# A hand-ordered attention and maxout-FFN kernel: its command list written in a new order, and its last branch laid out anew

## The chip, the cores and the metric

The kernel runs on one core of a Trainium2 chip. The metric is the device time of one execution in microseconds, lower is better. The kernel before ran three times: 202.09, 202.83 and 203.22 us, median 202.83. A profiled execution comes with it; "the profile" and "the trace" below are of that execution.

## The reference

Inputs are q, k, v of 4 batches x 8 heads x 768 positions x 64, a flag per head, and four weights, all float32.

```python
scores = scale * np.matmul(q, k.transpose(0, 1, 3, 2))
causal = rel >= 0                      # rel = query position - key position
stream_keep = causal & (is_sink | in_win)   # first 4 keys, or the last 64
mask = where(is_retrieval[head], causal, stream_keep)
a = softmax(where(mask, scores, -1e9))
x = (a @ v) -> [3072 tokens, 8 heads * 64 = 512]
h = max(x @ w1, x @ w2, x @ w3)        # three 512 x 768 matmuls, elementwise maximum
out = h @ w_out                        # 768 x 512
```

Heads whose flag is set (retrieval heads; 0, 2 and 6 in the data) attend to all earlier keys; the others to 4 sink keys and a window of 64. The result is 3072 x 512 float32.

## The kernel before

The kernel has two programs. The fast one is written for a guess of the flags, `GUESS = (1, 0, 1, 0, 0, 0, 1, 0)`. It also compares the real flags with the guess and checks that all softmax sums are within bounds; from both it makes one integer, `differ`. At its end every engine loads `differ` into a register and branches: if it is not zero, a general program computes everything again. In the data given it is zero, so the branch's body, `general()`, is never entered, but its instructions are there.

**The order.** The fast program is a list of commands, the string tuple `PROGRAM`. They are carried out in the order written; each issues a few instructions to the engines' queues, and each engine works off its own queue in order, waiting where data or buffers are not ready. So the list sets the order of the work on every engine, and letters in the commands (d, a, p: VectorE, ScalarE, GpSimd) set which engine does a copy, a cast or a mask. The commands:

- `hl half hp n`: loads of q and k of batch 0 for n head pairs, half a sequence each, by SP's DMA queue (line 185). `cast` (L199) makes them float16, `turnp` turns them by PE transposes (L217) and copies them to the tile KQ (L220).
- `load b quad`: loads of q and k of the later batches by GpSimd's DMA queue. `turn b quad i part` turns a quarter with one VectorE 32 x 32 transpose (L251); eight of them make a batch.
- `load_v b half` loads V by SP's queue; `v` (L436) and `y` (L448, L450) copy it as float16 to the tiles va and vx.
- `kx0` and `kx` (L476, L481, L488) gather far and sink keys. `cleark j` clears the two kx tiles of one parity (L465); `clear j` clears va's ones column and vx (L346 to L348).
- `strip n0 n1` copies mask blocks into the strip that masks are read from, 14 VectorE copies each (L333).
- `s0 half u pairs...` and `s b s`: score matmuls (L526, L597) into one of two PSUM buffers, and the exp on ScalarE (L546, L614). `k0` (L558) and `k` (L627) multiply a mask into the result, on VectorE or GpSimd.
- `av b half hp`: the attention times V for two heads (L646), reciprocal of the sums (L651) and scaling to x (L653) on VectorE. With D at the end, x goes transposed to xT by a DMA on SP's queue; without it, the command `x` does that by PE (L669) and a copy (L672).
- `w i`: a weight's load with a cast, by GpSimd's DMA queue (L361; w 3 is w_out).
- `f e`: one unit of the FFN. For each batch and half (384 tokens) there are 18 units of four matmuls (L387, a [128 x 384] block of one of the three products), whose result is copied to acc (L395) or taken as a maximum (L397), and 3 output blocks of six matmuls (L412), a copy (L418) and a store. For batch 0 all units of the first weight come first, then those of the second; later they alternate. The PSUM results of units, transposes and av share a ring of four banks.
- `flags`, `check`, `verdict` (L680 to L710): the comparison of flags, the check of sums, and the matmul and addition that write `differ`.
- `gs i` and `gp half hp`: tiny copies on SP's or GpSimd's queue that hold the queue until a weight or a load has landed. `idle n`: n matmuls on zeros (L295).

FFN units stand between the commands of the next batch's attention, so that PE always has something to do while the other engines prepare. L779 loads `differ`; L780 is the branch; rows of L941 belong to the closing behind it, where the engines wait for each other.

## Time and profile before

| | us |
|---|---|
| three runs, median | 202.83 |
| the profiled execution | 202.28 |
| its span, first to last instruction | 200.2 |
| PE busy | 180.6 |
| VectorE (DVE) busy | 152.4 |
| ScalarE (ACT) busy | 99.4 |
| GpSimd (POOL) busy | 72.3 |
| last matmul ends | 193.4 |
| first FFN unit on PE | 32.2 |

Times in the trace count from the first instruction of the span. A row of a group gives the source line, the engine, the operation, the tile written and the tile read, the number of instructions and either total and mean ns, or least, median and largest ns with the first and last start. A row of the waits reads: engine and tile that waited, what it waited for, us in total, how often, the longest. In a row of stretches each engine's busy us stands with its number of instructions; the last three columns are the clock granted to PE (1.00 is full), the mean busy share of the DMA engines, and GB/s.

### The profile page before, as it was taken

The numbers are of one execution on the slowest core, as the hardware profiler recorded it, in microseconds if no ns is written. First come the engines' busy times: TensorE is split into PE (matmuls) and PEld (weight loads), VectorE is DVE, ScalarE is ACT, GpSimd is POOL, SyncE is SP. The second block draws the span as 40 slices with busy tenths as digits, with TensorE's granted clock in tenths as the row PEclk, the third lists the DMA queues.
The fourth block names the chain that finished last, engine by engine and source line by source line (L and its number), as shares of the span: only waits on it lengthen the run. The fifth ranks groups of instructions, "written<-read, shape, count | busy, mean of one in ns | idle before, by whom it ended". The sixth has DMA issues, their size and how long they took to land.

```text
span 200.2 us, 4763 instructions
## 1 busy us (share of the span) xinstructions
PE 180.6 (90%) x1833; PEld 106.2 (53%) x1833; DVE 152.4 (76%) x357; ACT 99.4 (50%) x170; POOL 72.3 (36%) x111
## 2 busy tenths in 40 slices
PE   0297798999999999999999999999999999999960
PEld 0244365565555644567556645574566467655530
DVE  4897569999797899998479999793667469877800
ACT  2359758723867666174765584537556350000030
POOL 6134724446798215077092049013571030000000
PEclk9999559999999999999999999999999999999996
DMA  5999999999498958996498141014201511340040
GB/s 143 321 166 210 255 203 202 211 142 208 71 212 201 184 102 182 291 230 128 143 233 159 20 144 57 0 24 123 96 0 23 151 65 22 62 157 4 0 160 11
DMA packets 48424, 26.63 MB, mean 133 GB/s; under 512 B 37259, under 2 KB 43915, under 8 KB 48395
## 3 DMA queue, kind: packets, MB, share of 16 engines
...
## 4 chain that ended last, share of the span: by engine, by line
PE 71%; DVE 11%; DMA 8%; issue 3%; ACT 3%; SPq 2%; DVEq 0%; ACTq 0%
PE yy L387 39%; PE yy L412 11%; PE oacc L646 6%; PE st L597 6%; DMA qs<-in_q_dram 6%; PE yst L387 3%; DVE x L653 2%; DMA xT<-x 2%; DVE hT L397 2%; DVE KQ L251 2%; SPq L185 2%; PE st L526 1%; PE tr L217 1%; DVE acc L397 1%; PE yst L412 1%
## 5 line engine op out<-in xcount | busy, mean ns | idle before, releaser
L614 ACT ACTIVATE pt<-st 128x1024 f16<-128x1024 f32 (+2 forms) x51 | 43.5, 907 | 28.0 <-PE st L597 26.4
L627 POOL TENSOR_TENSOR pt<-pt,strip 128x512 f16<-128x512 f16 (+4 forms) x36 | 35.7, 1008 | 55.4 <-ACT pt L614 52.4
L387 PE MATMUL yy<-xT,w2t 128*128 128x384 f16 x180 | 36.0, 326 | 0.4 <-ACT ot L418 0.4
L387 PE MATMUL yy<-xT,w0t 128*128 128x384 f16 x180 | 35.8, 326 | 0.4 <-DMA xT<-x 0.2
L387 PE MATMUL yy<-xT,w1t 128*128 128x384 f16 x180 | 35.2, 326 | 0.2 <-DVE x L653 0.2
L397 DVE TENSOR_TENSOR acc<-yy,acc 128x384 f16<-128x384 f32 x45 | 24.9, 558 | 10.3 <-PE yy L387 4.7
L412 PE MATMUL yy<-woutt,hT 128*128 128x512 f16 (+1 forms) x138 | 31.4, 375 | 0.4 <-DVE hT L397 0.4
L397 DVE TENSOR_TENSOR hT<-yy,acc 128x384 f16<-128x384 f32 x45 | 24.6, 554 | 3.8 <-PE yy L387 1.6
L395 ACT CAST acc<-yy 128x384 f16<-128x384 f32 x26 | 12.4, 486 | 28.1 <-PE yy L387 28.1
L251 DVE STREAM_TRANSPOSE KQ<-kq 128x384 f32<-128x384 f32 x24 | 25.5, 1132 | 0.0
L387 PEld LDWEIGHTS <-w0t 128*128 128x128 f16 x192 | 18.1, 98 | 13.4 <-issue 1.0
L387 PEld LDWEIGHTS <-w1t 128*128 128x128 f16 x192 | 18.1, 98 | 12.9 <-issue 1.1
L387 PEld LDWEIGHTS <-w2t 128*128 128x128 f16 x192 | 17.5, 97 | 12.4 <-issue 1.3
L412 PEld LDWEIGHTS <-hT 128*128 128x128 f16 x150 | 14.0, 98 | 16.1 <-DVE hT L397 1.7
L546 ACT ACTIVATE pt<-st 128x1024 f16<-128x1024 f32 (+4 forms) x28 | 16.2, 636 | 10.1 <-PE st L526 9.8
L646 PEld LDWEIGHTS <-pt 128*128 128x128 f16 x472 | 18.0, 100 | 3.0 <-issue 0.4
L646 PE MATMUL oacc<-va,pt 128*128 128x65 f16 x392 | 19.0, 197 | 0.0
L653 DVE TENSOR_TENSOR x<-oacc,sums 128x384 f16<-128x384 f32 x32 | 17.8, 557 | 1.1
L627 DVE TENSOR_TENSOR pt<-pt,strip 128x256 f16<-128x256 f16 (+4 forms) x33 | 13.9, 437 | 5.6 <-ACT pt L614 5.6
L597 PE MATMUL st<-KQ 32*128 32x128 f16 (+2 forms) x342 | 15.1, 257 | 0.0
L597 PEld LDWEIGHTS <-KQ 32*128 32x128 f16 x342 | 8.8, 92 | 6.8 <-issue 5.6
L646 PE MATMUL oacc<-vx,pt 128*128 128x65 f16 x80 | 12.3, 193 | 0.0
...
## 6 DMA issues: line engine op xcount, KB each, us to landing
...
```

The costliest lines, as they stand in the source:

```text
L185: eng.dma_start(out=st[:, h : h + 2], in_=src[0, 2 * hp + h : 2 * hp + h + 2, half * HALF : (half + 1) * HALF].rearrange("h (p j) d -> p h ...
L251: nc.vector.transpose(out=dst.rearrange("c (p j) -> c j p", j=n)[:, j0:j1], in_=src.rearrange("c (j i) -> c j i", i=R),)
L387: nc.tensor.matmul(yy[:, 0:HALF], w_t[wi][:, ks, ni * P : (ni + 1) * P], xT[b, half, ks].rearrange("p a t -> p (a t)"), start=(ks == 0), s ...
L395: copy_out[0](out=acc[ni], in_=yy[:, 0:HALF])
L397: nc.vector.tensor_tensor(out=acc[ni] if wi == 1 else hT[ni], in0=yy[:, 0:HALF], in1=acc[ni], op=ALU.max)
L412: nc.tensor.matmul(yo[:, 0:n], hT[ns][:, tb * P : (tb + 1) * P], woutt[:, ns, c : c + n], start=(ns == 0), stop=(ns == NNB - 1),)
L546: nc.scalar.activation(out=pts[0, half, hp, u][:, r0:r1, c0:c1], in_=sts[hp][:, r0:r1, c0:c1], func=AF.Exp, scale=sc,)
L597: nc.tensor.matmul(sts["XY"[g // 2]][:, g % 2, c0 : c0 + n * P], KQ[rows, 0, ki * P : (ki + 1) * P] if kind == "p" else kx[b % 2][quad][ro ...
L614: nc.scalar.activation(out=pts[b, s, xy][:, r0:r1, c0:c1], in_=st[:, r0:r1, c0:c1], func=AF.Exp, scale=sc,)
L627: engine.tensor_tensor(out=x, in0=x, in1=m, op=ALU.mult)
L646: nc.tensor.matmul(o[:, i, r, 0 : D + 1], at[b, h, kind, ki, qi], vv[:, 0 : D + 1], start=(n == 0), stop=(n == len(todo) - 1), skip_group_ ...
L653: nc.vector.tensor_tensor(out=x, in0=o[:, :, :, 0:D], in1=rc.unsqueeze(3).to_broadcast([P, HB, 2, D]), op=ALU.mult,)
```

## The change

Three things change. The list is written anew: the same commands in another order, with engines of copies, casts and masks assigned anew, and the two `idle` commands at other places. A command `read` loads `differ` to a register of all five engines, and a command `hint` on all five announces the branch at the end with its register. And the branch is laid out the other way round: the empty arm, which is the one taken, no longer follows the branch directly with a jump past `general()` behind it; it stands behind `general()`, ahead of the closing, and is reached by the branch's own jump.

By letters: masks `k` on VectorE/GpSimd 33/36 before and 26/43 after; `k0` 9/8 and 1/16; `f` on ScalarE/VectorE 90/78 and 96/72; `v` on ScalarE/VectorE/GpSimd 11/11/10 and 9/13/10; `y` 5/12/10 and 10/6/11.

```diff
-    "clear 1, flags, hl 0 1 1 ss, clear 0, cast 0 0 pp, turnp 0 0 dd, cleark 0, hl 0 2 2 ss",
-    "strip 0 14, cast 0 2 aa, cast 0 1 ap, turnp 0 1 d, kx0 0 0 a, s0 0 0 0, hl 1 0 2 ss",
-    "cast 1 0 dd, turnp 0 2 ad, turnp 1 0 da, cleark 1, load_v 0 0 0 4, cast 1 1 ap, idle 2",
-    "kx0 0 1 a, s0 0 0 1, cast 0 3 dd, s0 0 1 0, s0 0 1 1, strip 14 28, kx0 1 0 p, load_v 0 0 4 4",
-    "v 0 0 3 d, hl 1 2 2 ss, v 0 0 2 d, turnp 0 3 aa, cast 1 2 dd, load 1 0, s0 1 1 0, s0 0 1 3",
...
-    "y 0 0 5:8:2 s d, s0 0 0 3, turnp 1 3 da, s0 0 0 2, turnp 1 2 da, k0 0 1 1 d, s0 1 3 1, w 0",
-    "kx0 1 3 d, v 0 0 1 p, x 0 0 0 a, av 0 0 3, y 0 0 4:5:1 r p, av 0 0 1, s0 1 0 1",
-    "y 0 0 4:5:1 s p, av 0 0 2, w 1, s0 1 1 3, w 2, turn 1 0 1 0, load_v 0 1, x 0 0 1 d",
...
-    "f a, load 1 1, turn 1 0 0 0, f d, f a, k0 1 0 0 d, kx0 1 2 p, s0 1 1 1, k0 1 0 1 d",
...
-    "f a, f a, f a, v 0 1 0 a, w 3, av 0 1 0 D, v 0 1 2 a, v 0 1 1 p, k0 3 3 0 p, av 0 1 1 D, f d",
-    "s0 1 2 3, k0 2 1 2 p, turn 1 1 0 0, s0 1 0 2, turn 1 1 0 1, k0 2 0 2 p, turn 1 1 1 0",
-    "turn 1 1 1 1, f d, v 0 1 3 a, idle 8, f d, f a, f a, s 1 1, load_v 1 0, k0 3 1 1 p, av 0 1 3",
...
-    "f d, f a, gp 1 2, k 3 5 X 0 d, av 3 1 2 D, f a, gs 0, f d, k 3 3 X 0 p, f d, av 3 1 0 D",
-    "av 3 1 1 D, f d, av 3 1 3 D, f d, f a, f a, f d, f d, f d, f d, f d, f d, f a, f a, f a, f d",
-    "f d, check, f d, f d, f a, f a, f a, f d, f d, f d, gs 1, verdict, f a, f a, f d, f a, f a",
+    "cast 0 0 aa, turnp 0 0 ad, hl 0 1 1 ss, clear 0, cleark 0, cast 0 1 aa, hl 0 2 2 ss",
+    "cast 0 2 da, load_v 0 0 0 4, kx0 0 0 a, s0 0 1 0, turnp 0 1 d, hl 1 0 2 ss, cast 1 0 dp",
+    "s0 0 0 0, turnp 0 2 da, s0 0 1 1, idle 8, w 0, kx0 0 1 d, cast 1 1 dp, cast 0 3 da",
+    "turnp 0 3 dd, y 0 0 1:4:2 r a, load 1 0, kx0 0 2 a, s0 0 0 2, load_v 0 0 4 4, kx0 0 3 p",
...
+    "turnp 1 0 da, clear 1, kx0 1 0 p, s0 0 0 3, av 0 0 0, s0 0 1 2, av 0 0 1, turnp 1 1 a, w 1",
+    "hl 1 2 2 ss, w 2, cast 1 3 pp, load_v 0 1, turnp 1 3 aa, x 0 0 1 d, cast 1 2 dd, kx0 1 1 p",
+    "s0 0 1 3, y 0 0 4:5:1 s a, s0 1 3 3, cleark 1, y 0 0 5:8:2 s p, gs 1, av 0 0 3, v 0 0 2 p",
+    "av 0 0 2, x 0 0 0 a, kx0 1 3 d, s0 1 0 1, x 0 0 3 a, strip 14 28, load 1 1, x 0 0 2 a",
+    "load_v 1 0, strip 0 14, s0 1 2 1, w 3, turnp 1 2 aa, kx0 1 2 d, k0 3 3 0 p, s0 1 0 3, f d",
...
+    "k0 3 1 1 p, f d, k0 3 0 1 p, idle 2, turn 1 1 0 1, turn 1 1 0 0, kx 1 1 a, k0 3 1 0 p",
+    "k0 2 0 2 p, k0 0 0 1 p, f d, gp 1 2, v 0 1 3 p, k0 3 0 0 p, f a, turn 1 1 1 0, turn 1 1 1 1",
...
+    "f a, s 2 1, k 2 1 X 1 p, turn 3 0 0 0, f a, av 1 1 0 D, turn 3 0 1 0, f d, av 1 1 3 D",
...
+    "k 3 6 Y 0 d, f a, k 3 4 X 1 d, f a, f d, flags, f d, f a, f a, f a, k 3 7 X 0 p, k 3 4 Y 0 p",
...
+    "f d, verdict, f d, f a, f a, read, hint, f a, f d, f d, f d, f d, f a, f a, f d, gs 0, f d",
+    "f d, f a, f a, f a, f a, f a, f a",
...
+    def read():
+        found["n"] = nc.values_load(differ[0:1, 0:1], min_val=0, max_val=1 << 20)
...
+        read=read,
+        hint=lambda: tc.mark_branch_hint_location("last", found["n"], [mybir.EngineType.SP, mybir.EngineType.PE, mybir.EngineType.Activation, mybir.EngineType.DVE, mybir.EngineType.Pool]),
...
-    return differ
+    return found["n"]
...
-        differ = fast(
+        n = fast(
...
-        n = nc.values_load(differ[0:1, 0:1], min_val=0, max_val=1 << 20)
-        with tc.If(n > 0, preferred_fallthrough_block=False):
+        with tc.If(n > 0, preferred_fallthrough_block=True, label="last"):
             general(tc, nc, q, k, v, is_retrieval, int(n_sink), int(window), w_t, woutt, out, xs_dram)
```

75 rows, old and new, of the table PROGRAM are left out of this document.

## Prediction, made before the changed kernel had run

> **What bounds the kernel now.** I read the page first: the shares of the engines and the chain that ended last.
>
> ```profile
> PE 180.6 (90%) x1833; PEld 106.2 (53%) x1833; DVE 152.4 (76%) x357; ACT 99.4 (50%) x170; POOL 72.3 (36%) x111
> ...
> PE 71%; DVE 11%; DMA 8%; issue 3%; ACT 3%; SPq 2%; DVEq 0%; ACTq 0%
> ```
>
> TensorE is the bound. The number of matmuls does not change, so only the time in which PE stands still, or runs at a lower clock, can be won or lost. The table of busy time in stretches tells where that is.
>
> ```profile
> 10.00:15.00 5.00, 4.76 (x30) 2.28 (x28) 4.89 (x16) 2.78 (x6) 1.73 (x4) 1.00 0.96 167
> 15.00:20.00 5.00, 3.59 (x38) 2.06 (x34) 3.52 (x18) 4.54 (x12) 2.32 (x6) 0.91 1.00 209
> 20.00:25.00 5.00, 3.99 (x31) 1.77 (x29) 2.67 (x7) 3.78 (x8) 3.82 (x7) 0.50 1.20 255
> 25.00:30.00 5.00, 4.93 (x52) 3.16 (x53) 3.15 (x11) 2.64 (x5) 1.06 (x3) 0.56 1.15 202
> ...
> 30.00:50.00 20.00, 19.50 (x209) 11.73 (x210) 19.68 (x41) 10.95 (x21) 9.94 (x16) 1.00 1.10 191
> ...
> 50.00:193.40 143.40, 142.02 (x1472) 83.81 (x1469) 111.26 (x235) 71.34 (x113) 49.48 (x64) 1.00 0.48 110
> ...
> 195.00:201.00 6.00, 0.00 (x0) 0.00 (x0) 0.00 (x0) 0.00 (x0) 0.00 (x0) 0.63 0.06 16
> ```
>
> Columns: stretch, length, then PE, PEld, DVE, ACT, POOL busy; last the granted clock, the DMA share, GB/s. Three things are to be seen. Before 30 us DMA is full (0.96 to 1.20) while no engine is. From 30 to 50 DVE has 19.68 of 20.00: it sets the pace. From 50 to 193.4 PE lacks 143.40 - 142.02 = 1.38 us, and after 195 nothing computes for 5.2 us. Why DVE enters its full stretch late is in the waits and in the weight's DMA:
>
> ```profile
> DVE qn L199 <- DMA qs<-in_q_dram: 3.7, 1, 3.7
> ...
> L361 POOL DMA_DIRECT2D w0t<-in_moe_w_dram x1: 816/816/816, 20.4 to 20.4; - x1
> ...
> DMA to landing us min/median/max: 9.5/9.5/9.5
> ...
> L251 DVE STREAM_TRANSPOSE KQ<-kq x8: 1097/1122/1161, 31.3 to 47.0; 128x384 f32<-128x384 f32 x8
> ...
> L333 DVE COPY strip<-kb x28: 129/181/600, 9.2 to 17.3; 128x128 f16<-128x128 f16 x28
> ```
>
> The first weight lands at 20.4 + 9.5 = 29.9; the eighth transpose of batch 1 ends at 47.0 + 1.1 = 48.1. The end is in the rows of the branch (line 780) and of the closing (line 941):
>
> ```profile
> L780 PEldq COMPARE_BRANCH  x2: 95/1892/3688, 191.2 to 193.5; - x2
> L780 SPq COMPARE_BRANCH  x2: 38/48/57, 193.5 to 195.8; - x2
> L780 ACTq COMPARE_BRANCH  x2: 38/44/49, 194.8 to 194.9; - x2
> ...
> L941 SPq EVENT_SEMAPHORE  x14: 17/28/28, 198.5 to 200.1; - x14
> ...
> L941 ACTq DRAIN  x2: 8/43/78, 195.4 to 199.6; - x2
> L941 PEldq DRAIN  x2: 8/40/73, 197.3 to 199.7; - x2
> ```
>
> SP jumps at 195.8 and does its next instruction at 198.5: 2.7 us with nothing between. PE's jump takes 3.7 (193.5 to 197.3). ACT jumps at 194.9 and goes on at 195.4: 0.5.
>
> The sums below start from the profiled execution, 202.28 us (span 200.2, 2.08 around it); the median of the runs is 202.83, 0.55 or 0.3% above it, and the runs go from 202.09 to 203.22, so the profiled one is of the quicker sort: I add 0.2 at the end.
>
> **The end.** The empty arm now stands just ahead of the closing, the jump into it is announced by the hint, and the second, unconditional jump goes. If the target is there when SP jumps, SP takes ACT's 0.5 in place of 2.7: 2.2 us. What SP does behind it (198.5 to 200.1) waits for PE's closing too, and PE's 3.7 was over at 197.3; if its jump shrinks alike, PE is done by 194.0 and holds nobody. The last output's landing (SP waits until 195.7) is untouched. No row shows a hint here. Ends: 0 (the target is fetched all the same) and 2.7 + 0.1 for the jump that goes; I take 2.3, nearest to ACT's row.
>
> The early **read** of the flag stands three units behind the verdict. In before DVE wrote the flag at 188.6, 0.7 after the verdict's matmul at 187.9, and a load of it took 0.49 on PE: 1.2 us, under which lie three units of 4 x 0.326 / 2 = 0.65, that is 1.95 (the chain shows 0.65 a unit). PE's load could be issued as soon as its queue reaches it, ahead of the matmuls that still wait, and then holds those behind it: bound 0 to 0.5, I take 0. On DVE (0.82) and ACT (0.48) the load is hidden by 190 to 195, where they are busy 0.46 and 1.54 of 5.
>
> **The start.** Removed from the early part: both strip fills and one clear (kx of batch 1). They go behind `x 0 0 1`, the turn of the second head pair for the FFN. The weight w0 is issued after the cast of the first pair of the second half, about 13 instead of 20.4, so it lands near 22.5 by its own 9.5. It no longer sets the first unit (32.2 in before); x does, and that needs the q of the last pairs of the second half, which landed at 22.2 (end of the 3.7 wait). POOL then casts k and q (0.51 each), PE turns them, ACT copies (0.48 each): `x 0 0 1` ends on DVE near 23.0. I follow DVE from there to the eighth transpose, in order, by the rows of before:
> - 8 transposes x 1.122 = 9.0; 12 FFN copies and maxima x 0.556 = 6.7; two of av (0.189 + 0.557) = 1.5; two casts x 0.54 = 1.1; two clears of kx x 0.485 = 1.0; four small copies and masks about 0.8: 20.1.
> - 28 strip copies: their two groups took 1.4 + 2.3 = 3.7 wall.
>
> Successive rows of DVE overlap: between 32.6 and 48.1 the durations sum to 17.0 in 15.6 us, so 20.1 counts 20.1 x 0.92 = 18.4. With 3.7 that is 22.1 us. In before DVE was idle for about 4 us between the landing at 22.2 and its eighth transpose (25 to 30 alone shows 1.85); there PE stood at clock 0.50 and they waited for each other. Now the strips and the clears, which wait for nobody, lie in that place; I leave 1.2 of idle. The eighth transpose then ends at 23.0 + 22.1 + 1.2 = 46.3, against 48.1, and PE's list ahead of it holds 16 units instead of 13 (+1.95), less two av's of two head pairs (2 x 0.62) and a score block (0.1): 0.6 more. Gain 1.8 + 0.6 = 2.4.
> Ends: if DVE idles 4 us as before, and x comes 1 us late, it is 2.4 - 2.8 - 1.0 = -1.4. On the good side landings bind: the last quarter of batch 1 landed at 42.3 and as many bytes stand ahead of it as before, so two transposes behind it end at 44.5: 4.2. w1 (34.5) and w2 (38.6) would be wanted near 34.5 and 39, just covered.
>
> **Queues.** SP is now held by its gate on w1 (to 34.5); behind it stand only the loads of V for batch 1, used past 47. POOL takes 16 of 17 masks of the first batch and 43 of 69 later (36 before), at 1.01 against 0.44 on DVE: POOL has 49.5 of 143.4 busy, so 7 us fit, and each takes 0.44 off DVE. A mask that is late holds an av by 0.6; I count nothing, up to +0.5.
>
> **The middle.** PE's 1.38 us of standing lie at 60 to 80 (0.83) and 100 to 120 (0.47), where the transposes of batches 2 and 3 fill DVE (14.74 of 16 from 64 to 80). The transposes are spread anew; the tightest place left is batch 1's second half, two av's with two transposes of batch 3 between them (2.2 on DVE under 1.3 of units). I take 0.5 won of the 1.38; ends +1.4 and -1.5 (that pair uncovered and one landing late).
>
> Sum: 202.28 - 2.3 - 2.4 - 0.5 = 197.1, and with the 0.2, **197.3**.
>
> [...]
>
> **Rivals.**
> 1. The hint brings nothing: the gap of 2.7 stays. For it: no row shows a hint working, and 15 units lie between it and the jump. Against: ACT, DVE and POOL jump in 0.5, so the target need not be far in itself. 197.3 + 2.3 = 199.6.
> 2. The start gains nothing: DVE idles as in before (4 us), 2.8 more: 197.3 + 2.8 = 200.1. For it: clock 0.50 and DMA 1.2 may hold in 20 to 30 as before. Against: the strips fill it.
> 3. Slower: w0 passes the last q and k of the second half on DMA. It has 512 x 768 x 4 B = 1.57 MB; at the 335 GB/s of the fullest stretch 4.7 us. If all of it goes ahead, x comes at 27.7, and with 4 us idle the eighth transpose ends at 53.8: 5.7 - 0.6 = 5.1 lost, 202.28 + 5.1 - 2.8 = 204.6. It decides once x and the idle time together come 5.2 us later than the forecast's 23.0 + 1.2, for then the 2.4, the 2.3 and the 0.5 are used up. Against: q and k go by SP's queue, w0 by POOL's, and they share.
> 4. Better: landings alone bind the start (4.2 in place of 2.4): 195.5.
>
> Both 1 and 2: 202.4, no change.
>
> **Chances.** Forecast 0.43, rival 1 0.16, rival 2 0.17, both 0.07, rival 3 0.12, rival 4 0.05. About 0.5% (1 us, 201.8 to 203.8) is what can be told from no change: faster 0.81, same 0.07, slower 0.12. The range runs from rival 4 with the end at its own bound (195.5 - 0.5 = 195.0) to the two failures together (202.4); outside lie rival 3 and a little below.
>
> **What would show it.** End: SP's closing semaphores within 1 us of its second-last branch row, PE's within 1 us too; else rival 1. Start: w0 issued near 13 and landed by 23; `x 0 0 1` on DVE by 23; eighth transpose by 46.3; PE full from there. Rival 3: the wait of the cast for qs ends past 25. Middle: PE busy in 50 to its last matmul within 0.9 of that stretch. What would make me wrong most: a cold clock for longer than 19 to 29, or DVE's long stretch idling on landings.

## The result, and the profile after

The changed kernel took 214.18 us (median of 4 runs, 213.44 to 215.35), the kernel before 202.81 beside it: a ratio of 1.0567, interval 1.0536 to 1.0598. It is 11.4 us slower where 197.3 was forecast, and outside of the range. The profiled execution took 215.35, its span is 213.6. (In e7, e10, e13 and e18 below some executions were over 1.5% longer than the fastest of their kernel; the ratios leave those out, so there they do not agree with the medians, and the traces of e10 and e18 are of such executions.)

The page of the kernel after, its busy times and the shares of the chain that ended last:

```profile
PE 183.2 (86%) x1833; PEld 105.9 (50%) x1833; DVE 143.4 (67%) x337; ACT 101.5 (48%) x175; POOL 86.4 (40%) x126
...
PE 67%; DMA 18%; DVE 7%; SPq 2%; issue 2%; ACT 1%; POOL 1%; POOLq 0%; DVEq 0%
```

TensorE has the same 1833 matmuls and is busy 2.6 us longer with them (some ran at a lower clock: in the units of the first weight up to 0.528 us instead of 0.326). DVE's share of the chain fell from 11% to 7%, as one would expect from the masks that left it. But DMA's rose from 8% to 18%: what is new on the chain is transfers. The chain names them by line (first row), and its longest pieces by start and length:

```profile
by line: PE yy L388 40.6%; DMA qs<-in_q_dram 9.8%; PE yy L413 9.1%; DMA xT<-x 7.8%; PE oacc L647 5.3%; PE st L598 5.2%; DVE KQ L252 2.9%; PE yst L388 2.8%; issue 1.6%; PE st L527 1.4%; SPq L186 1.1%; DVE x L654 1.1%; SPq L275 0.9%; DVE hT L
...
15.32 13.38 DMA qs<-in_q_dram
57.74 10.36 DMA xT<-x
```

Two transfers: one load of q that took 13.4 us, and one DMA transpose of x that took 10.4. Both are to be found in the busy times by stretches (columns as in the prediction):

```profile
15.00:20.00 5.00, 4.21 (x62) 2.64 (x60) 4.50 (x14) 4.31 (x8) 3.73 (x7) 1.00 1.06 201
20.00:25.00 5.00, 0.50 (x3) 0.24 (x3) 0.46 (x1) 1.18 (x3) 0.50 (x1) 0.61 1.10 227
25.00:30.00 5.00, 0.58 (x6) 0.59 (x7) 0.00 (x0) 0.05 (x1) 1.02 (x3) 0.50 1.15 210
30.00:35.00 5.00, 4.76 (x47) 2.68 (x44) 4.48 (x18) 3.90 (x9) 3.70 (x7) 0.50 1.17 208
...
60.00:80.00 20.00, 14.92 (x149) 7.79 (x151) 8.57 (x18) 10.20 (x15) 6.90 (x7) 0.83 0.84 153
...
140.00:160.00 20.00, 18.24 (x223) 11.20 (x220) 13.14 (x31) 10.94 (x18) 7.22 (x7) 1.00 0.22 61
```

From 20 to 30 PE does 1.08 of 10 us (before: 8.92, at half clock), and no other engine does more than a fifth either: everybody waits, with DMA full. PE's granted clock is 0.50 until 38.1 (its row from 30 to 35 shows 4.76 us of work at 0.50). From 60 to 80 PE lacks 5.1 us (before 0.8). From 140 to 160 it lacks 1.8 (before nothing). What PE waited for in the first 70 us, the longest two:

```profile
PE tr L218 <- POOL qn L200: 5.7, 1, 5.7
PE yy L388 <- DMA xT<-x: 5.1, 1, 5.1
```

**The first hole.** The loads of q by SP's queue and the weights' DMAs on POOL's:

```profile
L186 SPq DMA_DIRECT2D qs<-in_q_dram x7: 368/467/469, 2.2 to 15.3; - x7
...
DMA to landing us min/median/max: 3.6/4.5/13.4
```

```profile
L362 POOL DMA_DIRECT2D w0t<-in_moe_w_dram x1: 962/962/962, 13.4 to 13.4; - x1
...
L362 POOL DMA_DIRECT2D w1t<-in_moe_w_dram x1: 747/747/747, 17.9 to 17.9; - x1
...
L362 POOL DMA_DIRECT2D w2t<-in_moe_w_dram x1: 755/755/755, 18.6 to 18.6; - x1
```

The last q was issued at 15.3, as in before (15.6), and landed at 28.7; in before the q that VectorE waited for landed at 22.2, and the last one was there by 24.5, when its cast began without a wait. All three weights are issued by 18.6; in before none of them was before 20.4. So `x 0 0 1` ends at 30.6 and the first FFN unit starts at 36.3 (32.2 in before), although w0 had landed at 22.9. Between 0 and 60 us the copy of `x 0 0 1` on DVE waited for its turn on PE:

```profile
DVE xT L673 <- PE tr L670: 9.8, 1, 9.8
```

That turn does not read the late q. What it reads, the scaled x of the second head pair, was written by DVE at 20.5. But in the list `turnp 1 3`, the turn of that q, stands ahead of `x 0 0 1`, and PE did them in that order: the turn of q at 29.41, that of x at 29.71. So the q holds the first unit by its place in the queue alone.

**The second hole**, 63.08 to 68.15: the DMA transposes of x for the second half, and the loads of batch 2's k and q on POOL's queue:

```profile
L660 SPq DMA_TRANSPOSE xT<-x x3: 1267/1267/1468, 57.7 to 60.7; - x3
...
DMA to landing us min/median/max: 8.2/9.1/10.4
```

```profile
L237 POOL DMA_DIRECT2D kq<-in_k_dram x3: 530/549/596, 55.8 to 57.4; - x3
L237 POOL DMA_DIRECT2D kq<-in_q_dram x3: 525/545/548, 56.4 to 58.4; - x3
```

The six loads were issued from 55.8 on, the last one at 58.4, the transposes at 57.7, 59.3 and 60.7. The last load landed at 67.90, and the transposes at 68.11, 68.45 and 68.84. The first transpose even landed behind two loads that were issued 0.2 and 0.7 us after it (they landed at 65.51 and 67.90). In before the loads were spread from 52.9 to 63.7, and the transposes were quicker:

```profile
L236 POOL DMA_DIRECT2D kq<-in_k_dram x3: 524/556/598, 52.9 to 62.7; - x3
L236 POOL DMA_DIRECT2D kq<-in_q_dram x3: 497/520/536, 53.5 to 63.7; - x3
...
L659 SPq DMA_TRANSPOSE xT<-x x5: 1181/1206/1966, 52.2 to 73.1; - x5
...
DMA to landing us min/median/max: 2.3/3.9/4.6
```

**The end:**

```profile
L785 SPq EVENT_SEMAPHORE  x7: 17/17/17, 211.5 to 211.9; - x7
...
L785 PEldq COMPARE_BRANCH  x1: 417/417/417, 204.8 to 204.8; - x1
...
L785 SPq COMPARE_BRANCH  x1: 73/73/73, 208.2 to 208.2; - x1
```

PE's jump shrank from 3.7 to 0.42. SP's did not: 208.2 to 211.5, 3.3 us. But SP now jumps while the last output is still on its way (landed by 211.0), so only 0.5 to 0.8 of it shows, counted from that landing. From the last matmul (207.6) to the end of the span there are 6.0 us; in before 200.2 - 193.4 = 6.8.

### The profile page after: what moved, and what is told of

Same layout as the page of the kernel before. It is cut to its first block, busy times and chain, and to the rows that moved or that the text cites. A ratio compares the mean times of both kernels' runs of the same rounds, so it can differ in the third digit from the quotient of the medians.

```text
span 213.6 us, 4761 instructions
## 1 busy us (share of the span) xinstructions
PE 183.2 (86%) x1833; PEld 105.9 (50%) x1833; DVE 143.4 (67%) x337; ACT 101.5 (48%) x175; POOL 86.4 (40%) x126
## 4 chain that ended last, share of the span: by engine, by line
PE 67%; DMA 18%; DVE 7%; SPq 2%; issue 2%; ACT 1%; POOL 1%; POOLq 0%; DVEq 0%
PE yy L388 41%; DMA qs<-in_q_dram 10%; PE yy L413 9%; DMA xT<-x 8%; PE oacc L647 5%; PE st L598 5%; DVE KQ L252 3%; PE yst L388 3%; PE st L527 1%; SPq L186 1%; DVE x L654 1%; SPq L275 1%; DVE hT L398 1%; PE yst L413 1%; ACT pt L547 1%
## 5 line engine op out<-in xcount | busy, mean ns | idle before, releaser
L628 POOL TENSOR_TENSOR pt<-pt,strip 128x512 f16<-128x512 f16 (+5 forms) x43 | 43.2, 1022 | 62.4 <-ACT pt L615 62.1
L388 PE MATMUL yy<-xT,w0t 128*128 128x384 f16 x180 | 38.7, 344 | 7.1 <-DMA xT<-x 7.1
L388 PE MATMUL yy<-xT,w1t 128*128 128x384 f16 x180 | 35.7, 326 | 0.0
L388 PE MATMUL yy<-xT,w2t 128*128 128x384 f16 x180 | 35.5, 326 | 0.1
L396 ACT CAST acc<-yy 128x384 f16<-128x384 f32 x32 | 15.4, 482 | 38.9 <-PE yy L388 32.9
L398 DVE TENSOR_TENSOR acc<-yy,acc 128x384 f16<-128x384 f32 x45 | 24.9, 560 | 12.3 <-PE yy L388 8.8
L647 PEld LDWEIGHTS <-pt 128*128 128x128 f16 x472 | 17.9, 99 | 5.3 <-issue 1.2
L647 PE MATMUL oacc<-va,pt 128*128 128x65 f16 x392 | 19.6, 196 | 1.0 <-ACT pt L547 1.0
L654 DVE TENSOR_TENSOR x<-oacc,sums 128x384 f16<-128x384 f32 x32 | 17.9, 558 | 1.2
L559 POOL TENSOR_TENSOR pt<-pt,strip 128x128 f16<-128x128 f16 (+3 forms) x16 | 12.6, 815 | 6.5 <-ACT pt L547 3.9
L396 DVE CAST acc<-yy 128x384 f16<-128x384 f32 x13 | 7.2, 555 | 11.3 <-PE yy L388 11.3
L419 ACT COPY ot<-yy 128x512 f32<-128x512 f32 x14 | 8.1, 588 | 12.0 <-PE yy L413 8.5
```

Source lines behind the costliest of these rows:

```text
L388: nc.tensor.matmul(yy[:, 0:HALF], w_t[wi][:, ks, ni * P : (ni + 1) * P], xT[b, half, ks].rearrange("p a t -> p (a t)"), start=(ks == 0), s ...
L396: copy_out[0](out=acc[ni], in_=yy[:, 0:HALF])
L398: nc.vector.tensor_tensor(out=acc[ni] if wi == 1 else hT[ni], in0=yy[:, 0:HALF], in1=acc[ni], op=ALU.max)
L559: engine.tensor_tensor(out=x, in0=x, in1=m if r < 2 else m.to_broadcast([P, 2, n, P]), op=ALU.mult)
L628: engine.tensor_tensor(out=x, in0=x, in1=m, op=ALU.mult)
L647: nc.tensor.matmul(o[:, i, r, 0 : D + 1], at[b, h, kind, ki, qi], vv[:, 0 : D + 1], start=(n == 0), stop=(n == len(todo) - 1), skip_group_ ...
```

## The experiments

The theory after the result: three weights issued early take the DMA from the last loads of the second half (the first hole), and the loads of batch 2 take it from the transposes (the second). Rivals: one of the two is enough; the later order of the list or the new engines cost by themselves; DVE's strips behind `x` set the start; the new end costs.

### Each hole by itself

**e1: only w0 later**

```diff
-    "s0 0 0 0, turnp 0 2 da, s0 0 1 1, idle 8, w 0, kx0 0 1 d, cast 1 1 dp, cast 0 3 da",
+    "s0 0 0 0, turnp 0 2 da, s0 0 1 1, idle 8, kx0 0 1 d, cast 1 1 dp, cast 0 3 da",
...
-    "turnp 1 0 da, clear 1, kx0 1 0 p, s0 0 0 3, av 0 0 0, s0 0 1 2, av 0 0 1, turnp 1 1 a, w 1",
+    "turnp 1 0 da, clear 1, kx0 1 0 p, s0 0 0 3, av 0 0 0, s0 0 1 2, av 0 0 1, turnp 1 1 a, w 0, w 1",
```

> The changed kernel (214.2) with one command moved: the load of w0 goes from behind the cast of the first pair to just ahead of the load of w1, behind the loads of the last q and k of the second half. Theory (w0 goes ahead of those q and k on DMA and makes them land late): the last q lands by about 23 in place of 28.7, PE's hole of 5.7 us at 23.8 to 29.4 is gone or under 1 us, and the time falls by 4 to 6, to 208 to 210. Rival (they are late because three loads of V now stand ahead on SP's own queue): the landing stays at 28 to 29 and the time at 213 to 215.

Measured: 214.55 us, 1.0536 (1.0464 to 1.0609): no gain that can be told. The last q took 10.9 instead of 13.4 and landed at 25.6, and the first unit started at 33.2 instead of 36.3. But little of it was left at the end: at the transposes PE now stood for 6.1 us instead of 5.1. So w0 is a part of the first hole, and to mend that part alone brings nothing that can be told.

**e2 and e3: the loads of batch 2 later in the list.** e2 moves both halves of them behind the last av of the first half and its turn; e3 only the second half.

```diff
-    "av 0 1 3, load 2 0, v 0 1 0 a, av 0 1 0 D, load 2 1, v 0 1 2 a, s 1 1, k 1 1 X 0 p",
-    "k 1 1 X 1 d, av 0 1 1 D, av 0 1 2 D, x 0 1 3 d, f d, s 1 0, k 1 0 X 0 d, load_v 1 1",
+    "av 0 1 3, v 0 1 0 a, av 0 1 0 D, v 0 1 2 a, s 1 1, k 1 1 X 0 p",
+    "k 1 1 X 1 d, av 0 1 1 D, av 0 1 2 D, x 0 1 3 d, f d, load 2 0, load 2 1, s 1 0, k 1 0 X 0 d, load_v 1 1",
```

> The changed kernel with both loads of batch 2 moved from ahead of the three DMA transposes of batch 0's second half to behind them and one FFN unit. Theory (a DMA transpose lands only after all loads that were issued before it): the transposes land within 4 us of their issue (10.4 in the changed kernel), PE's hole of 5.1 us at 63.1 to 68.2 is gone, and the time falls by 4 to 5, to 209 to 210. Rival (the DMA engines are simply full, whatever the order): a hole of some 3 to 5 us stays at that place or opens a little later, where batch 2 is turned: 212 to 214.

The edit of e3, against the kernel after:

```diff
-    "av 0 1 3, load 2 0, v 0 1 0 a, av 0 1 0 D, load 2 1, v 0 1 2 a, s 1 1, k 1 1 X 0 p",
-    "k 1 1 X 1 d, av 0 1 1 D, av 0 1 2 D, x 0 1 3 d, f d, s 1 0, k 1 0 X 0 d, load_v 1 1",
+    "av 0 1 3, load 2 0, v 0 1 0 a, av 0 1 0 D, v 0 1 2 a, s 1 1, k 1 1 X 0 p",
+    "k 1 1 X 1 d, av 0 1 1 D, av 0 1 2 D, x 0 1 3 d, f d, load 2 1, s 1 0, k 1 0 X 0 d, load_v 1 1",
```

> As the run before, but only the second load of batch 2 (four DMAs of the six) is moved behind the transposes. If a transpose waits for whatever was issued ahead of it, it lands just behind the last piece of the first load (62.9 in the changed kernel), so about 63 to 64, and the hole shrinks from 5.1 to 0 to 1: 209.5 to 210.5. If it only shares the DMA engines with what is under way at any time, the moved load, issued 3 us later, still slows it: a hole of 2 to 4 us and 211 to 213.

Measured: e2 218.5, 1.0742 (1.0681 to 1.0803); e3 215.87, 1.0678 (1.0607 to 1.075). Neither is better than the kernel after (1.0567), and e2 is worse. The loads of k in e2, by the tile that they write, and the transposes by theirs:

```profile
L237 POOL DMA_DIRECT2D kq<-in_k_dram x3: 530/549/596, 58.6 to 60.2; - x3
```

```profile
DMA to landing us min/median/max: 2.4/6.8/10.1
```

The loads had moved in the list, but hardly in time: POOL had nothing ahead of them that waits, so it ran ahead of PE and issued them at 58.6 to 61.2, now between the three transposes (57.5, 58.9, 60.2). The first transpose, issued 1.1 us ahead of the first load, took 2.4; the second, between the loads, 6.8; the third 10.1. In e3 the first, issued 0.03 us ahead of a load, took 5.9, and the second and third 10.4 and 9.3. So e2 is no test of "loads away". e3 was to tell whether a transpose waits only for loads issued ahead of it, for then they had to land by 63 to 64: they landed at up to 68.2, so that is not so. The forecast for sharing (211 to 213, with PE standing for 2 to 4) missed as well: PE stood for 5.9.

**e5: the loads behind an instruction that waits.** `k 1 2 X 0 p` is a mask on POOL that needs a result of PE.

```diff
-    "av 0 1 3, load 2 0, v 0 1 0 a, av 0 1 0 D, load 2 1, v 0 1 2 a, s 1 1, k 1 1 X 0 p",
+    "av 0 1 3, v 0 1 0 a, av 0 1 0 D, v 0 1 2 a, s 1 1, k 1 1 X 0 p",
...
-    "v 1 0 1 a, v 1 0 2 p, f a, k 1 0 X 1 d, f d, s 1 2, k 1 2 Y 0 d, f a, k 1 2 X 0 p, f a, f a",
+    "v 1 0 1 a, v 1 0 2 p, f a, k 1 0 X 1 d, f d, s 1 2, k 1 2 Y 0 d, f a, k 1 2 X 0 p, load 2 0, load 2 1, f a, f a",
```

> The changed kernel with both loads of batch 2 behind a mask of batch 1 on POOL's queue, which waits for an exp (its mask started at 64.3), so that they are issued near 65 and not between the transposes as in the two runs before, where POOL ran ahead. Theory (a DMA transpose lands only behind all that was issued before it): all three transposes land 2 to 4 us after their issue, by 65; PE's hole of 5.1 us at 63 is gone or under 0.7; 209 to 210.5, if nothing later waits for the loads (first needed at 78). Rival (the full DMA engines set it): the hole comes back at the turns of batch 2 or at the later transposes, 212 to 215.

Measured: 211.3, 1.0392 (1.0308 to 1.0476). The loads were issued near 65, and the transposes:

```profile
L660 SPq DMA_TRANSPOSE xT<-x x3: 1179/1207/1312, 57.4 to 60.1; - x3
...
DMA to landing us min/median/max: 2.3/2.3/2.4
```

The second hole is gone, and its cause is shown: the loads of batch 2 beside the transposes. The gain is 1.75% (3.5 us) and not 5, and a new hole of 2.3 us stands at 71.1, behind a copy of V on DVE that took 3.95 us (see e7).

**e6: the three weights behind the casts of the last pair of the second half**, that is, once its q has landed.

```diff
-    "s0 0 0 0, turnp 0 2 da, s0 0 1 1, idle 8, w 0, kx0 0 1 d, cast 1 1 dp, cast 0 3 da",
+    "s0 0 0 0, turnp 0 2 da, s0 0 1 1, idle 8, kx0 0 1 d, cast 1 1 dp, cast 0 3 da",
...
-    "turnp 1 0 da, clear 1, kx0 1 0 p, s0 0 0 3, av 0 0 0, s0 0 1 2, av 0 0 1, turnp 1 1 a, w 1",
-    "hl 1 2 2 ss, w 2, cast 1 3 pp, load_v 0 1, turnp 1 3 aa, x 0 0 1 d, cast 1 2 dd, kx0 1 1 p",
+    "turnp 1 0 da, clear 1, kx0 1 0 p, s0 0 0 3, av 0 0 0, s0 0 1 2, av 0 0 1, turnp 1 1 a",
+    "hl 1 2 2 ss, cast 1 3 pp, w 0, w 1, w 2, load_v 0 1, turnp 1 3 aa, x 0 0 1 d, cast 1 2 dd, kx0 1 1 p",
```

> The changed kernel with the loads of all three first weights behind the cast that waits for the last q and k of the second half. Theory (not w0 alone but the three weights, 4.7 MB issued by 19.4 us, share DMA with these q and k): the last q lands at 22 to 23.5 (28.7 in the changed kernel, 25.6 with w0 moved alone), x is turned by 25, the first unit starts near 33 to 34 as w0 lands about 33, against 36.3; the hole at 20 to 29 shrinks by 5 us. If the hole at 63 stays as it is: 209 to 211; if it takes the gain back, because the loads of batch 2 are then issued earlier against the transposes, as with w0 moved alone: 212 to 214. Rival (V's loads ahead on SP's queue hold q): q lands at 25 or later, 213 to 215.

Measured: 213.79, 1.0504 (1.0423 to 1.0584); by the intervals that is not told apart from the kernel after. The loads of q and PE's longest waits:

```profile
DMA to landing us min/median/max: 3.6/4.9/8.9
```

```profile
PE yy L388 <- DMA xT<-x: 5.9, 1, 5.9
PE tr L218 <- POOL qn L200: 4.2, 1, 4.2
```

With no weight beside it the longest q takes 8.9 and lands at 24.0. So the last q took 13.4 with w0 issued at 13.4, 10.9 with all three weights issued after 17.7 (e1), and 8.9 with none beside it. The first unit starts at 32.4 instead of 36.3; and the wait at the transposes is 5.9 us long instead of 5.1, as in e1. The price is that the weights now land late, at 31.8, 35.4 and 39.4.

**e7: e5 and e6 together**

> The two edits before together. If these are the two causes of the loss and do not share a cause, the time falls by the sum of theirs, to 203.5 to 206; what is left over 202.8 less the shorter end is the new order's own. If something else in the start (clock, strips on DVE) costs as much: 207 or more.

Measured: 208.54, 1.0239 (1.0158 to 1.032). By the ratios e5 took 1.75% off, e6 0.6%, both 3.3%. Each is uncertain by some 0.8, so that they are worth more together than singly is not shown by the times; e6's trace, with its longer wait at the second hole, is what speaks for it. The time is still above the forecast of 203.5 to 206, so something else costs as well. A new hole of PE stands at 67.5 (2.3 us). A small copy of V on DVE, and the masks on POOL between 64 and 70:

```profile
L449 DVE CAST vx<-vs x1: 3964/3964/3964, 65.2 to 65.2; 64x128 f16<-64x128 f32 x1
```

```profile
L628 POOL TENSOR_TENSOR pt<-pt,strip 128x512 f16<-128x512 f16 (+2 forms) x4 | 4.5, 1149 | 0.0
```

The copy took 3.96 us, where the same copy takes 0.22 elsewhere. During it POOL ran four masks one directly behind the other, from 65.3 to 69.7; the copy, begun at 65.2, ended at 69.2, half a microsecond before the recorded end of the last of them (as in e5).

**e10: e7 with that copy on ScalarE**

```diff
-    "y 1 0 4:5:1 r d, k 1 0 Y 0 p, f d, av 1 0 0 D, load_v 2 0, f d, turn 2 0 0 0, s 1 5, f a",
+    "y 1 0 4:5:1 r a, k 1 0 Y 0 p, f d, av 1 0 0 D, load_v 2 0, f d, turn 2 0 0 0, s 1 5, f a",
```

> The kernel with both edits (e7, 208.5) and one copy of V (64 x 128, y 1 0 4:5:1 r) on ScalarE in place of VectorE. In e7 this copy took 3.96 us on VectorE at 65.3, 0.22 in the changed kernel, while GpSimd ran four masks end to end from 65.3 to 69.7, and PE then stood 2.3 us. Theory (VectorE was shut out by GpSimd's masks, which holding the loads had moved there): without the copy no VectorE row there is over 1 us, PE's hole at 67.5 is gone, 206 to 207. Rival (chance of this row, or another VectorE operation is shut out in its place): a hole of 1 to 2.5 us stays near there, 207.5 to 209.

Measured: 205.84, 1.0127 (1.0084 to 1.017). The copy takes 0.3 on ScalarE, the hole at 67.5 is gone, and PE is busy 20.00 of 20.00 from 60 to 80. One letter is worth 1.1% by the middle of the two ratios, 2.3 us; their intervals just meet (1.0158 and 1.017), so the hole that is gone from the trace, 2.3 us too, says it more surely than the times. The same four masks ran here (66.0 to 70.5). That masks on POOL do not hold all of DVE's work is seen in the kernel after: its 32 scalings to x, which read PSUM, took 0.557 to 0.559 us each, three of them wholly beside masks. With the two holes and the one that opened behind them taken out, 1.3% of the 5.7% remain.

**e4: the kernel before, with w0 issued early and nothing else**

```diff
-    "cast 1 0 dd, turnp 0 2 ad, turnp 1 0 da, cleark 1, load_v 0 0 0 4, cast 1 1 ap, idle 2",
+    "cast 1 0 dd, turnp 0 2 ad, turnp 1 0 da, cleark 1, load_v 0 0 0 4, cast 1 1 ap, w 0, idle 2",
...
-    "y 0 0 5:8:2 s d, s0 0 0 3, turnp 1 3 da, s0 0 0 2, turnp 1 2 da, k0 0 1 1 d, s0 1 3 1, w 0",
+    "y 0 0 5:8:2 s d, s0 0 0 3, turnp 1 3 da, s0 0 0 2, turnp 1 2 da, k0 0 1 1 d, s0 1 3 1",
```

> The kernel before (202.8) with one command moved, the load of w0 put where the change has it, behind the early casts of the second half (issued near 12 in place of 20.4). Theory (w0 delays the last q and k): these land 4 to 6 us later than 22.8, the first FFN unit starts later than 32.2 although its weight is there earlier, and the time rises by 3 to 5, to 206 to 208. Rival (the order of the rest is what costs): 202 to 204, as the weight comes earlier and q and k as before.

Measured: 204.98, 1.0118 (1.0073 to 1.0163). The weight and the first unit:

```profile
L361 POOL DMA_DIRECT2D w0t<-in_moe_w_dram x1: 952/952/952, 12.0 to 12.0; - x1
```

```profile
L387 PE MATMUL yy<-xT,w0t x24: 323/326/337, 35.0 to 40.1; 128*128 128x384 f16 x24
```

w0 lands at 19.3 instead of 29.9, the q that VectorE waits for at 25.0 instead of 22.2, the first unit starts at 35.0 instead of 32.2, later by the same 2.8, and the kernel is 2.4 us slower. The order of the kernel before, q first and w0 5 us behind it, is the better one; this is the step of the prediction tried alone, and it has the other sign.

### Start, rest, strips, clock

**e13 and e14: the two halves of the list crossed.** e13 has the list of before through `x 0 1 3 d` (near 58 us) and the remaining commands of after; e14 the list of after through that command, and the rest of before with the new end.

> The kernel before's list up to the turn of the last x of batch 0, and from there the new list with its end, each command once. In the traces PE's lost time against a full clock grew in the changed kernel by 8.9 us more up to 60 us and by 5.1 in the hole of the transposes; from 70 us on both lists gain alike. Theory (the whole loss lies in the start and in the loads of batch 2 against the transposes, the rest is worth as much as before): 200.5 to 203, with loads of batch 2 that may still meet the one last transpose. Rival (the rest of the new list, with 43 masks on GpSimd, costs something of its own): 204 to 208.

> The reverse: the new list up to the turn of the last x of batch 0 (with the first loads of batch 2, which lie in it), from there the list of before with the new end as in e8. Theory: nearly all of the loss, 212 to 215. Rival: 206 or less.

Measured: e13 205.43 (scattered, 202.76 to 210.77), 1.0085 (1.0047 to 1.0122); e14 214.96, 1.0621 (1.0586 to 1.0657). The loss comes with the first part of the list: e14 has all of it, with the wait for q (7.2) and that for the transposes (3.8), whose loads belong to that part. Of the new rest 0.85% can be told, although it has the new end, and in its trace one mask on DVE stands out:

```profile
L628 DVE TENSOR_TENSOR pt<-pt,strip x4: 291/500/5300, 53.1 to 59.2; 128x512 f16<-128x512 f16 x2, 128x256 f16<-128x256 f16 x1, 128x1024 f16<-128x1024 f16 x1
```

The one of 128 x 1024 took 5.30 us (59.2 to 64.5), where this shape takes some 0.8 elsewhere; POOL ran masks from 58.5 to 63.9, and PE stood for 2.6 behind it. It looks like what e7 showed, at another place; no run moved it away.

**e15: the kernel before, with the strips, the clear and two masks behind `x 0 0 1`** (the place of the strips in the kernel after).

```diff
-    "strip 0 14, cast 0 2 aa, cast 0 1 ap, turnp 0 1 d, kx0 0 0 a, s0 0 0 0, hl 1 0 2 ss",
-    "cast 1 0 dd, turnp 0 2 ad, turnp 1 0 da, cleark 1, load_v 0 0 0 4, cast 1 1 ap, idle 2",
-    "kx0 0 1 a, s0 0 0 1, cast 0 3 dd, s0 0 1 0, s0 0 1 1, strip 14 28, kx0 1 0 p, load_v 0 0 4 4",
+    "cast 0 2 aa, cast 0 1 ap, turnp 0 1 d, kx0 0 0 a, s0 0 0 0, hl 1 0 2 ss",
+    "cast 1 0 dd, turnp 0 2 ad, turnp 1 0 da, load_v 0 0 0 4, cast 1 1 ap, idle 2",
+    "kx0 0 1 a, s0 0 0 1, cast 0 3 dd, s0 0 1 0, s0 0 1 1, kx0 1 0 p, load_v 0 0 4 4",
...
-    "y 0 0 4:5:1 s p, av 0 0 2, w 1, s0 1 1 3, w 2, turn 1 0 1 0, load_v 0 1, x 0 0 1 d",
+    "y 0 0 4:5:1 s p, av 0 0 2, w 1, s0 1 1 3, w 2, turn 1 0 1 0, load_v 0 1, x 0 0 1 d, cleark 1, strip 14 28, strip 0 14, k0 0 1 0 p, k0 0 1 1 d",
```

> The kernel before (202.8) with the strips, the clear of the far keys of batch 1 and the two masks that need the strip moved behind the turn of x of the second pair, as the change has them. VectorE is full from 30 to 50 us, so work of 3.7 + 1.0 us put at 32 has no cover there. Prediction's step (the strips fill time in which VectorE waited): 202 to 203.5. Rival (they lengthen the full stretch): 2 to 4.5 us more, 205 to 207.5.

Measured: 215.34, 1.062 (1.059 to 1.0651). It looks like the kernel after, but for another reason. The waits of POOL and of PE:

```profile
POOL pt L558 <- DVE strip L333: 10.4, 1, 10.4
```

```profile
PE st L526 <- POOL kx L476: 4.4, 1, 4.4
```

A mask on POOL's queue waited 10.4 us for the late strip, and a copy of kx that PE needed was queued behind it. So it is no clean test of DVE's load, and nothing is concluded from it about the strips.

**e17 and e16: the strips and the clear early**, ahead of the turn of pair 1 where DVE is empty (20 to 25). e17 does it in the kernel after, e16 in e10.

```diff
-    "s0 0 1 3, y 0 0 4:5:1 s a, s0 1 3 3, cleark 1, y 0 0 5:8:2 s p, gs 1, av 0 0 3, v 0 0 2 p",
-    "av 0 0 2, x 0 0 0 a, kx0 1 3 d, s0 1 0 1, x 0 0 3 a, strip 14 28, load 1 1, x 0 0 2 a",
-    "load_v 1 0, strip 0 14, s0 1 2 1, w 3, turnp 1 2 aa, kx0 1 2 d, k0 3 3 0 p, s0 1 0 3, f d",
+    "s0 0 1 3, y 0 0 4:5:1 s a, s0 1 3 3, y 0 0 5:8:2 s p, gs 1, av 0 0 3, v 0 0 2 p",
+    "av 0 0 2, x 0 0 0 a, kx0 1 3 d, s0 1 0 1, x 0 0 3 a, load 1 1, x 0 0 2 a",
+    "load_v 1 0, s0 1 2 1, w 3, turnp 1 2 aa, kx0 1 2 d, k0 3 3 0 p, s0 1 0 3, f d",
...
-    "turnp 1 0 da, clear 1, kx0 1 0 p, s0 0 0 3, av 0 0 0, s0 0 1 2, av 0 0 1, turnp 1 1 a, w 1",
+    "turnp 1 0 da, clear 1, kx0 1 0 p, s0 0 0 3, av 0 0 0, s0 0 1 2, av 0 0 1, strip 14 28, strip 0 14, cleark 1, turnp 1 1 a, w 1",
```

> The changed kernel (214.2) with only the strips and that clear put ahead of the wait for the last q. VectorE stands there from 20.5 to 30.3, so they cost nothing. Theory: lost time at 55 us falls by 3 to 4.7; but the loads of batch 2 then meet the transposes as before, and the hole at 63 takes back a part as it did when w0 alone was moved: 210 to 213. Rival (strips don't matter): 213.5 to 214.8.

> The kernel with three edits (e10, 205.8: weights behind q, loads of batch 2 held, one copy off VectorE), and the strips with the clear of the far keys of batch 1 put ahead of the wait for the last q, where VectorE had nothing to do from 20 to 25 us (0.12 of 5.0 busy). Theory (their 3.7 + 1.0 us lengthen VectorE's stretch, as in the old list with the strips late): the eighth transpose of batch 1 ends 3 to 4.7 us earlier than in e10, and the time falls by 2.5 to 4.5, to 201.3 to 203.3. Rival (ScalarE's exps, 8.8 of 10 busy in 30 to 40, or the weights' landings set the stretch): less than 1 us, 205 to 206.

Measured: e17 214.91, 1.0597 (1.0562 to 1.0631); e16 205.86, 1.015 (1.012 to 1.018). No gain in the time of either. In e17 the eighth transpose of batch 1 did end sooner, at 53.6 instead of 55.5, but PE then stood for 5.5 us at the transposes of x. In e16, without that hole, it ended at 52.7, against 52.4 in e10. The stretch from 30 to 35 in e16:

```profile
30.00:35.00 5.00, 5.00 (x34) 2.29 (x30) 1.17 (x4) 4.38 (x9) 1.97 (x4) 0.50 1.15 209
```

DVE is now nearly free there (1.17), and nothing is won by it: PE is busy all the time, at clock 0.50. So in e10 the strips behind `x` are not what binds the start. In the kernel after itself they may cost the 1.9 us by which e17's eighth transpose came sooner, but the second hole took that back.

**e9: e7 with the clock held**: 24 matmuls on zeros where PE would wait for q.

```diff
-    "hl 1 2 2 ss, cast 1 3 pp, w 0, w 1, w 2, load_v 0 1, turnp 1 3 aa, x 0 0 1 d, cast 1 2 dd, kx0 1 1 p",
+    "hl 1 2 2 ss, cast 1 3 pp, w 0, w 1, w 2, load_v 0 1, idle 24, turnp 1 3 aa, x 0 0 1 d, cast 1 2 dd, kx0 1 1 p",
```

> The kernel with both edits (e7, 208.5) and 24 matmuls on zeros put ahead of the turn that waits for the last q (5.2 us of PE at full clock, in a hole of 5.3 us from 19.5 to 24.8). In e7 the granted clock is 0.5 from about 21 to 34.5, and PE is busy 3.9 of 5 and 5.0 of 5 in 25 to 35. Theory (the hole costs a second time, by the lower clock behind it): the clock stays at 1.00, the first FFN unit starts near 30 to 31 in place of 32.5, and the time falls by 2 to 4, to 204.5 to 206.5. Rival (VectorE with the strips, 33.0 of 45 busy, or the landing of the weights at 31.8, 35.4 and 39.3 sets the pace): the clock stays up and the time falls by less than 1.

Measured: 209.98, 1.0329 (1.0281 to 1.0377), no gain on e7's 1.0239.

```profile
25.00:30.00 5.00, 3.01 (x44) 1.99 (x44) 3.52 (x9) 2.73 (x8) 4.89 (x10) 1.00 0.97 159
30.00:35.00 5.00, 4.57 (x29) 1.97 (x28) 4.42 (x32) 4.16 (x9) 2.24 (x4) 0.57 1.16 211
```

The clock is 1.00 to 30, and PE, being quicker, waits (busy 3.01 of 5); from 30 on it is at 0.57 all the same. But the first unit starts at 32.7, once w0, which landed at 32.6, is there, so the clock could win little here. The run does not weigh the low clock, and whether it costs anything by itself stays open.

**e18: e16 with the 24 idle matmuls, and two copies of V on POOL ahead of the last casts**

```diff
-    "hl 1 2 2 ss, cast 1 3 pp, w 0, w 1, w 2, load_v 0 1, turnp 1 3 aa, x 0 0 1 d, cast 1 2 dd, kx0 1 1 p",
-    "s0 0 1 3, y 0 0 4:5:1 s a, s0 1 3 3, y 0 0 5:8:2 s p, gs 1, av 0 0 3, v 0 0 2 p",
+    "hl 1 2 2 ss, y 0 0 5:8:2 s p, v 0 0 2 p, cast 1 3 pp, w 0, w 1, w 2, load_v 0 1, idle 24, turnp 1 3 aa, x 0 0 1 d, cast 1 2 dd, kx0 1 1 p",
+    "s0 0 1 3, y 0 0 4:5:1 s a, s0 1 3 3, gs 1, av 0 0 3",
```

> The kernel with three edits and early strips (e16, 205.9), 24 matmuls on zeros in the hole ahead of the last q, and two copies of V on GpSimd put ahead of the cast that waits for q and of the issue of the weights, where av of the fourth pair waited 0.9 us for one of them. In e16 PE is busy 5.0 of 5 at clock 0.50 from 30 to 35, VectorE only 1.2 of 5; in the run with the clock alone (e9) VectorE with the strips was the bound there. Theory (the strips and the low clock hide each other, either one alone is enough to hold the start): the clock stays at 1.00 to 30 at least, the first unit starts when w0 lands (31.8) or before 32.3, the lost time at 55 us falls by 2 or more, and the time to 203 to 204.5. Rival (the weights' landings at 31.8, 35.6 and 39.7 and the exps set the start): less than 1 us, 205 to 206.5.

Measured: 207.27 as the median of 4 (203.71, 206.94, 207.6 and 207.85), against 202.64 for the kernel before beside it. They lie too far apart to say whether it gained on e16. The trace, of the execution that took 207.6, has the next bound, though:

```profile
PE yy L388 <- DMA w0t<-in_moe_w_dram: 1.9, 1, 1.9
```

The clock is 1.00 until 30, `x` is ready, and the first unit starts at 32.0, when w0, issued at 25.2, lands. With q first, the weights bind the start; with the weights first, q does. In before w0 is issued between the two, at 20.4.

### The end

**e8, e11, e12: the kernel before with the new end alone.** e8 has check, verdict and read earlier and the new order of the arms; e11 puts the hint's command three units ahead of the end; e12 has no hint.

```diff
-    "av 3 1 1 D, f d, av 3 1 3 D, f d, f a, f a, f d, f d, f d, f d, f d, f d, f a, f a, f a, f d",
-    "f d, check, f d, f d, f a, f a, f a, f d, f d, f d, gs 1, verdict, f a, f a, f d, f a, f a",
+    "av 3 1 1 D, f d, av 3 1 3 D, f d, f a, f a, f d, check, f d, f d, f d, f d, f d, verdict, f a, f a, f a, read, hint, f d",
+    "f d, f d, f d, f a, f a, f a, f d, f d, f d, gs 1, f a, f a, f d, f a, f a",
...
-        with tc.If(n > 0, preferred_fallthrough_block=False):
+        with tc.If(n > 0, preferred_fallthrough_block=True, label="last"):
```

> The kernel before with the new end alone: check and verdict earlier, then the load of the flag, the hint 15 FFN units ahead of the end, and the empty arm behind the general program. Prediction's step: SP's jump is short (0.5 in place of 2.7), 2.2 us won, 200.5. As the changed kernel's trace reads (SP branches at 208.2, still waits 3.3 us, but beside the output's landing, and PE's last matmul to the end of the span is 6.0 in place of 6.8): 0.8 to 1.0 won, 201.8 to 202.2. Rival (nothing): 202.5 to 203.

The edits of e11 (first) and e12 (second), against e8:

```diff
-    "av 3 1 1 D, f d, av 3 1 3 D, f d, f a, f a, f d, check, f d, f d, f d, f d, f d, verdict, f a, f a, f a, read, hint, f d",
-    "f d, f d, f d, f a, f a, f a, f d, f d, f d, gs 1, f a, f a, f d, f a, f a",
+    "av 3 1 1 D, f d, av 3 1 3 D, f d, f a, f a, f d, check, f d, f d, f d, f d, f d, verdict, f a, f a, f a, read, f d",
+    "f d, f d, f d, f a, f a, f a, f d, f d, f d, gs 1, f a, f a, hint, f d, f a, f a",
...
-    "av 3 1 1 D, f d, av 3 1 3 D, f d, f a, f a, f d, check, f d, f d, f d, f d, f d, verdict, f a, f a, f a, read, hint, f d",
+    "av 3 1 1 D, f d, av 3 1 3 D, f d, f a, f a, f d, check, f d, f d, f d, f d, f d, verdict, f a, f a, f a, read, f d",
```

> The kernel before with the new end (e8, 201.6), the hint only three FFN units ahead of the end in place of fifteen. In e8 SP branches at 194.4 and does its next instruction at 197.6, 3.2 us, 1.3 behind the output's landing. If the hint fetches the target and fifteen units displace it: SP goes on within 0.6 us of the last output's landing, 0.7 to 1.3 us less than e8, 200.3 to 201. If the hint does nothing in either place: as e8, 201.3 to 202.

> The same with no hint at all, the flag read early and the empty arm behind the general program. If the layout alone (jump beside the output's landing, one jump less) brings what e8 won: SP's step from branch to next instruction stays at 3 to 3.5, the time at 201.3 to 202. If the hint brought it: PE's or SP's step grows to 3.7 or more, and the time goes back to 202.3 to 203.3.

Measured: e8 201.62 (10 runs), 0.9928 (0.9896 to 0.996); e11 202.07 (12 runs), 0.9955 (0.9935 to 0.9975); e12 201.98 (12 runs), 0.9954 (0.9931 to 0.9977). In e11 the hint's rows stand directly behind the load of the flag, as in e8: its place in the list does not move it, so e11 is e8 once more. The rows of the branch in e8 and in e12:

```profile
L784 SPq EVENT_SEMAPHORE  x7: 17/17/17, 197.6 to 198.0; - x7
...
L784 PEldq COMPARE_BRANCH  x1: 417/417/417, 191.3 to 191.3; - x1
...
L784 SPq COMPARE_BRANCH  x1: 73/73/73, 194.4 to 194.4; - x1
```

```profile
L784 SPq EVENT_SEMAPHORE  x7: 17/17/17, 197.9 to 198.4; - x7
...
L784 PEldq COMPARE_BRANCH  x1: 3768/3768/3768, 190.8 to 190.8; - x1
...
L784 SPq COMPARE_BRANCH  x1: 53/53/53, 194.0 to 194.0; - x1
```

The hint takes PE's jump from 3.77 to 0.42, and SP's step, from its jump to its next row, from 3.9 to 3.2. Neither can be told in the time: PE jumps while its last matmuls still run, SP while the last output is on its way (landed at 196.4 and 197.3 in e8). The gain of 0.45 to 0.7% is left for the rest of the change, the earlier flag and one jump on the path in place of two behind each other; which of these brings it was not taken apart, and what the hint is worth by itself is below what these runs tell. The old list with the new end is the fastest version measured (e8 and e12, which can't be told apart), ahead of both kernels.

## Why the prediction was wrong

**The start** is the step that failed. It said that `x` "needs the q of the last pairs of the second half, which landed at 22.2", and took that landing over from the trace of before, while the same step moved w0 ahead of it. w0's own forecast held: issued 13.4 (about 13), landed 22.9 (22.5). But q landed at 28.7, `x` ended at 30.6 and not at 23.0, and the first unit came 4.1 us later than in before instead of earlier. Rival 3 had named the mechanism and put it at 0.12, with "they share" against it. To share was the harm: q took 13.4 us beside the weights, 8.9 without (e6), and e4 shows the sign with w0 alone. The rival was also too small, since it counted w0 only; w1 and w2, issued at 17.9 and 18.6 instead of 22.5 and 23.2, were in the list and in no term. (Its 335 GB/s is that of 4 us: from 6 to 10 the trace of before has 336; the fullest 5 us have 321, which makes its 4.7 us 4.9.) Nor does `x` need that q for its data, as the prediction had it; it stands behind the turn of q in PE's queue. A list with `x 0 0 1` ahead of that turn was not tried.

The last q took 13.4 us with w0 early, 10.9 with all weights later (e1) and 8.9 with none beside it (e6): the longer, the more weight traffic there was beside it on another queue.

**The rest of the start's sum.** The sum of 22.1 + 1.2 us from `x` to the eighth transpose of batch 1 came out as 24.9, of the right size; the end of it was at 55.5 and not at 46.3, nearly all because `x` was 7.6 late. The reason given for the gain, that DVE's idle place would take the strips, is not borne out: they stood behind `x` as well, DVE was busy 0.46 of the 10 us from 20 to 30, and e16 and e17, which put the strips there, were no faster. The start is not the whole miss of 16.9 us: e7, which mends both holes, takes back 3.3%, some 6.7 us.

**Queues.** This step looked at SP's gate and at V, and not at where the six loads of batch 2 come to stand beside the transposes of x, though before's list has them apart. It cost 5.1 us of standing (e5 removes it). "I count nothing, up to +0.5" for more masks on POOL asked whether POOL has the time, and not what a run of masks on POOL does to DVE. In the kernel after itself that cost nothing that its trace shows: the longest copy of V on DVE there, beside four masks in a row, took 1.42 us instead of 0.42. It came to light once the loads were moved: a copy of 0.22 us took 3.95 in e5 and 3.96 in e7, and moving it away closed a hole of 2.3 us in e10.

The copy of e7 and e5 ended 0.5 us before the end of POOL's masks, while in the kernel after the scalings to x, which read PSUM, took 0.557 to 0.559 us beside masks as elsewhere. The longest operations of DVE beside masks took 3.96 (e7) and 5.30 us (e13). What sets apart those that take so long, no run shows.

**The middle**: won 0.5 was forecast; from 80 to the last matmul PE stood for 2.15 us (127.6 less 125.45 busy), 1.8 of it for another DMA transpose of x, issued at 150.6. That hole stayed in the mended versions (2.1 in e10), and no run took it out.

**The end**: -2.3 was forecast, and 0.8 was seen after, 0.9 to 1.5 in e8 and its repeats. ACT's row was the wrong model for SP: SP's step stayed at 3.2 to 3.9, hint or not. Rival 1 said the hint brings nothing, and as to the time it was right, for what e12 wins without a hint can't be told from what e8 wins with it. What brought the gain, the earlier flag or the one jump that runs beside the output's landing, was not taken apart; no case of the prediction had the jump beside the landing. PE's jump did shrink: 3.77 unannounced (e12), 0.42 when it was announced 9.7 us ahead (e8, 181.6 and 191.3). That SP's gap is a wait for the jump's target was the author's assumption and is not shown; why SP's step did not shrink alike stays open.

**What stays open.** e10 still has 1.3% more than before, and some 2% more than e8. The late weights are one bound there (e18), with the hole at 144 to 153 another; how the rest divides is not settled. How the loads hold the transposes stays open too: in the kernel after they land 0.2 to 0.9 us behind the last load, but they also wait for loads issued after them (there and in e3), so an order of issue alone is not the reason. And no run moved `x 0 0 1` ahead of the turn of the late q, which may be the simplest way past the first hole.
